# A second MLP on one core: another order of transfers, and the remainder's units at two fixed places

## Chip, core and metric

The kernel runs on one core of a Trainium2 chip. The metric is the device time of one execution in microseconds (us). Three runs of the kernel before gave 961.51 us (median), 959.44 and 965.2 us.

## What is computed

Windowed attention with 32 global tokens in each of 4 batches and 8 heads gives 2176 token rows of 512 features. A gated MLP (RMS norm, 512 to 1536 to 512) and a second MLP follow:

```python
h = x @ w_in                     # 512 -> 2048
g = np.maximum(0.01 * h, h)
return (g @ w_out).astype(np.float32)   # 2048 -> 512
```

All of it is float32. To keep that accuracy each operand of a large product is split into a rounded high half (ScalarE cast) and a residual (VectorE subtract), and a product is three matmuls: high by high, low by high, high by low (`mm3`).

## The kernel before, in words

The change lies in the second MLP, the last 360 us or so. Its 2176 columns are 128 left over ("the rest") and two halves `s` of 1024. A half takes 8 up steps `up`, `j` = 0 to 7, one for each pair of hidden chunks, and then 8 down steps `dn`; 32 steps `g` in all.

An up step makes four blocks of hidden values by seven products of six matmuls each instead of eight (Strassen's scheme in Winograd's form). They run in the order 1, 6, 7, 5, 2, 4, 3. TensorE writes them to PSUM tiles `px`, `pw`, `py`, `pz`; VectorE adds them up (`u`, `v`, `h`), ScalarE copies `x` and applies the leaky ReLU (once on `h[:, 0]` behind product 2, once on the other three blocks behind product 3). Between the products the same engines prepare the next step's weights (`make_w`, places 0 to 2). In half 0 these are 128x768 and 128x1024 splits of `q`, which VectorE first extends by four sums; the finished operands `wr` (1792 KB) are also stored to DRAM (`keep_parts`), and half 1 loads them back (`fetch_w`). In a down step `make_w` splits the raw output weights, and `dop_of` splits the hidden values that are the stationary operands `d`. A `dop` ring of six buffers serves `d` and the rest's weights `rw`.

The rest is worked on in 32 units beside the up steps: unit `u` loads 256 KB (`rest_load`, two `raw` buffers), splits them into `rw` (`rest_split`), and multiplies with three matmuls into `pr` or `po` (`rest_step`). Units 0 to 15 are its first layer, with a turn of four transposes behind every fourth; units 16 to 31 its second, for which every fourth unit also needs a split of the rest's hidden values, `hr`.

The order on TensorE, VectorE, ScalarE and the SP queue is that of the code in this part (a manual schedule). Before it a scheduler places instructions. All transfers go out from SP in program order. An SP transfer whose source or buffer isn't ready holds up those behind it.

Before, `BESIDE` says how many units run in an up step (none in the first, three in the next two, then two), part of them behind product 7 and part behind product 4. A unit ends with the split of the unit two later and the load of the one four later. Behind product 4 SP gets the store of the next operands and then the load of a later `q`. In half 0 the columns for half 1 are loaded (`columns_in`) at the end of a down step and split (`columns_made`) at the end of the next.

Of the kernel before, what the change touches and what calls it, by code (L numbers as in the profile page):

```python
# [24 lines left out]
def tile_window_global_attention_two_mlps(  # L25
# [595 lines left out]


    PAIRS = NF2 // 2
    pre2, rings, ys2, w_in, w_out = [], [], {}, {}, {}

    def rows(c0, n):

# [55 lines left out]
    def keep_parts(j):  # L683
        nc.sync.dma_start(out=w2_dram[j], in_=w_in[0, j].bitcast(F32).rearrange("p y s c -> p y (s c)"))

    def quarter():
        return pre2[0].tile([P, 8, HK], F32, tag="q", name="q")

    def weight_pair(j):

        raws = []

        def make():
            q = quarter()
            for s, f, r in zip((0, 2), (j + PAIRS, j), raws):
                v = q[:, s:s + 2].rearrange("p s c -> p (s c)")
                narrow(mp, v, r, f"b0_{f}")
                nc.sync.dma_start(out=w2_f32[f][0], in_=v)
            weight_sums(q)
            for hi, lo, r in weight_parts(j):  # L700
                split(hi, lo, q[:, r])
            keep_parts(j)
        return [lambda: raws.extend(raw2(f, 0) for f in (j + PAIRS, j)), make]
# [23 lines left out]
    def ahead():  # L727

        ph_at.close()
        pre2.append(ctx.enter_context(tc.tile_pool(name="pre2", bufs=1, side="right", reuse_waits="tile")))  # L730

        jobs = one_ahead([narrowed(f, 0) for j in range(1, PAIRS - 4) for f in (j, j + PAIRS)] + [weight_pair(0)])
        for x, (k, d) in enumerate((k, d) for k in range(KC // 2) for d in range(0, HALF, HK)):
            jobs.insert(2 + 2 * x, lambda k=k, d=d: columns_made(0, k, d, columns_in(0, k, d)))
        return jobs

    def columns_in(s, k, d):

# [153 lines left out]
    rings.extend((pre2[0], wp2))  # L892
    ND = 6
    NU = 2 * NS * PAIRS
    wq, wfs, dops, hid = {}, {}, {}, {}

    def lone(name):

# [6 lines left out]
    def kind(g):  # L905
        s, r = divmod(g, 2 * PAIRS)
        return (s, *divmod(r, PAIRS))

    def load_q(j):

        if j < PAIRS:
            q = wq[j] = quarter() if j % 2 else wp2.tile([P, 8, HK], F32, tag=f"h{PAIRS - 1}", name=f"q{j}")
            for s, f in ((0, j + PAIRS), (2, j)):
                nc.sync.dma_start(out=q[:, s:s + 2].rearrange("p s c -> p (s c)"), in_=w2_f32[f][0])

    def fetch_w(g):

# [13 lines left out]
    def make_w(g, place):  # L931

        if g >= NU:
            return
        s, layer, j = kind(g)
        if layer:
            if place == 0:
                high(w_out[g][:, 0], wfs[g])
            elif place == 1:
                low(w_out[g][:, 1], wfs[g], w_out[g][:, 0])  # L940
        elif s == 0:
            q = wq[j]
            if place == 0:
                wq["parts"] = weight_parts(j)
                high(wq["parts"][0][0], q[:, wq["parts"][0][2]])
                weight_sums(q)
            elif place == 1:
                low(wq["parts"][0][1], q[:, wq["parts"][0][2]], wq["parts"][0][0])
                high(wq["parts"][1][0], q[:, wq["parts"][1][2]])
            else:  # L950
                low(wq["parts"][1][1], q[:, wq["parts"][1][2]], wq["parts"][1][0])
                keep_parts(j)
                load_q(j + 2)


# [23 lines left out]

    def rest_load(u):  # L980

        if u >= NRU + NF2:
            return
        raw = rest["raw", u] = wp2.tile([P, HALF], F32, tag="raw", bufs=2, name=f"raw{u}")
        if u < NRU:
            fq, kc = divmod(u, KC)
            nc.sync.dma_start(out=raw.rearrange("p (f c) -> p f c", c=P), in_=w2_fours[fq][:, :, kc * P:(kc + 1) * P])
        else:
            nc.sync.dma_start(out=raw, in_=w2_f32[u - NRU][1])

    def rest_split(u):

        if u < NRU + NF2:
            t = rest["w", u] = halves_tile(f"rw{u}")
            split(t[:, 0], t[:, 1], rest.pop(("raw", u)))
            rest_load(u + 2)

    def rest_cols(u):

        if NRU <= u < NRU + NF2 and u % 4 == 0:  # L1000
            t = rest["h"] = wp2.tile([P, 2, 4, P], F32R, tag="yr", name=f"hr{u}")
            split(t[:, 0], t[:, 1], rest["hid"][:, u - NRU:u - NRU + 4])

# [4 lines left out]
    def rest_second():  # L1008
        rest["y"] = wp2.tile([P, 2, KC, P], F32R, tag="yr", name="yr")
        split(*(rest["y"][:, h].rearrange("p k c -> p (k c)") for h in range(2)), rest["y32"])  # L1010
        rest["hid"] = wp2.tile([P, NF2, P], F32, tag="hid", name="hid")
        rest_split(0)
        rest_split(1)

    def rest_third():
        rest_cols(NRU)
        rest_split(NRU)
        rest_split(NRU + 1)

    def rest_turn(fq, hn):  # L1020
        pt = lone(f"pt{fq}")
# [4 lines left out]
    def rest_step(u):  # L1026
        w = rest.pop(("w", u))
        turn = rest.pop("turn", None)
        if u < NRU:
            fq, kc = divmod(u, KC)  # L1030
            if kc == 0:
                rest["p"] = lone(f"pr{fq}")
            mm3(rest["p"], [rest["y"][:, h, kc] for h in range(2)], [w[:, h] for h in range(2)], kc == 0, kc == KC - 1)
            if kc == KC - 1:
                hn = wp2.tile([P, HALF], F32, tag="hn", name=f"hn{fq}")
                leaky(hn, rest["p"])
                rest["turn"] = (fq, hn)
        else:
            f = u - NRU
            if f == 0:  # L1040
                rest["p"] = lone("po")
            mm3(rest["p"], [rest["h"][:, h, f % 4] for h in range(2)], [w[:, h] for h in range(2)], f == 0, f == NF2 - 1)
            if f == NF2 - 1:
                ob = wp2.tile([P, DM], F32, tag="hn", name="obr")
                nc.scalar.copy(ob, rest["p"])
                store_rows(0, ob)
        if turn:
            rest_turn(*turn)
        if u < NRU - 2 or u >= NRU:
            rest_cols(u + 1)  # L1050
            rest_split(u + 2)

    units = [lambda u=u: rest_step(u) for u in range(NRU + NF2)]


    BESIDE = {0: (0, 3, 3, 2, 2, 2, 2, 2), 1: (2,) * 8}

    def rest_run(s, j, place):

        n = BESIDE[s][j]  # L1060
        for _ in range(n // 2 if place else n - n // 2):
            units.pop(0)()


    SLOTS = ((0, 0), (0, 1), (1, 0), (1, 1))

# [7 lines left out]

    def up(g):
        s, _, j = kind(g)
        fetch_w(g + 1)
        h = hid[s, j] = wp2.tile([P, 4, HALF], F32, tag=f"h{j}", name=f"h{s}_{j}")
        x1, u2, v = [wp2.tile([P, HALF], F32, tag=x, name=f"{x}{s}_{j}") for x in ("x1", "u2", "v")]
        bx, bw, by = [bank(f"p{c}{s}_{j}") for c in "xwy"]  # L1080
# [4 lines left out]
        product(s, j, 7, by)  # L1085
        plus(v, u2, by)
        make_w(g + 1, 0)
        rest_run(s, j, 0)
        bz = bank(f"pz{s}_{j}")
        product(s, j, 5, bz)  # L1090
        plus(h[:, 3], v, bz)
        make_w(g + 1, 1)
        product(s, j, 2, bx, False)
        leaky(h[:, 0], bx)
        if j == PAIRS - 1:
            dop_of(s, 0)
            dop_of(s, 1)
        product(s, j, 4, by, False)
        plus(h[:, 1], u2, by)
        make_w(g + 1, 2)  # L1100
        if (s, j) == (0, 0):
            rest_second()
        rest_run(s, j, 1)
        product(s, j, 3, bz, False)
        plus(h[:, 2], u2, bz)
        leaky(h[:, 1:4], h[:, 1:4])

    def out_tile(s, t, last):
        ob = wp2.tile([P, DM], F32, tag=("x1", "u2", "v")[t % 3], name=f"ob{s}_{t}")
# [6 lines left out]
    def dn(g):  # L1116
# [6 lines left out]
        def unit(t, x):  # L1123
# [2 lines left out]
            mm3(dn.op[t], [d[:, h, t % 4 * P:(t % 4 + 1) * P] for h in range(2)], [w_out[g][:, h, f] for h in range(2)],  # L1126
                (j, f) == (0, 0), (j, f) == (PAIRS - 1, 1))

        if j < PAIRS - 1:
            for x, (f, n) in enumerate(SLOTS):  # L1130
                dop_of(s, 4 * j + x + 2)
                if x == 2:
                    make_w(g + 1, 0)
                for t in range(4 * n, 4 * n + 4):
                    unit(t, x)
                if x == 2:
                    make_w(g + 1, 1)
        else:
            for x in (2, 3):
                dop_of(s, 4 * j + x)  # L1140
            if s == 0:
                rest_third()
            make_w(g + 1, 0)
            for n, t in enumerate(range(NT2 - 1, -1, -1) if s else range(NT2)):
                for x in range(4):
                    if SLOTS[x][1] == t // 4:
                        unit(t, x)
                out_tile(s, t, n)
        if s + 1 < NS and 1 <= j < 6:
            if j > 1:  # L1150
                columns_made(*dn.columns)
            if j < 5:
                k, d = divmod(j - 1, 2)
                dn.columns = (s + 1, k, d * HK, columns_in(s + 1, k, d * HK))

    with tc.manual_schedule(engines={mybir.EngineType.PE, mybir.EngineType.DVE, mybir.EngineType.Activation,
                                     mybir.EngineType.SP}):
        load_q(1)
        load_q(2)
        rest_first()  # L1160
        rest_load(0)
        rest_load(1)
        for g in range(NU):
            (dn if kind(g)[1] else up)(g)

# [58 lines left out]
```

## Time and profile before

| | us |
|---|---|
| median of three runs | 961.51 |
| profiled execution | 963.23 |
| its span, first to last instruction | 961.5 |
| TensorE busy | 925.0 (96%) |
| VectorE busy | 585.5 (61%) |
| ScalarE busy | 461.0 (48%) |

The profile lists instructions by engine (PE is TensorE, DVE VectorE, ACT ScalarE, SP SyncE with the queue) with start and duration, and for idle time what ended it. TensorE's weight loads have a line of their own (PEld). A matmul's end is modelled; the step from one matmul's start to the next shows the pace.

### The profile page before, as it was taken

The page shows a single profiled execution, that of the slowest core. Times are in us where ns is not written, and L with a number is a line of the kernel's source. Part 1 is how long each engine was busy: PE and PEld are TensorE (multiplying, and loading weights), DVE is VectorE, ACT ScalarE, POOL GpSimd, SP SyncE. Part 2 cuts the span into 40 slices and gives each one's busy share as a digit, 9 for nine tenths or more (in the row PEclk, how much of TensorE's full clock was granted, in tenths as well). Part 3 has the DMA queues.
Part 4 walks back from the last instruction along what each step waited for, and adds up shares of the span by engine and source line. Part 5 has one row for each costly group of instructions (what it writes and reads, how often), then busy time and mean ns, then how long its engine had stood idle before and what let it go on. Part 6 is the DMA issues. An engine that isn't in the chain of part 4 may idle for free.

```text
span 961.5 us, 14038 instructions
## 1 busy us (share of the span) xinstructions
PE 925.0 (96%) x5056; PEld 755.1 (79%) x5056; DVE 585.5 (61%) x1216; ACT 461.0 (48%) x958; POOL 4.5 (0%) x26
## 2 busy tenths in 40 slices
PE   6799999999999999999999999899999999999998
PEld 4557777777777777777999999778788788888886
DVE  5689985596666887443577833666545634445332
ACT  5886774664554655333454422455433523434222
POOL 1000000000000000000000000000000000000000
PEclk9899999999999999999999999999999999999999
DMA  9587994876769999744789992678422275641113
GB/s 306 174 283 262 312 365 149 276 271 228 254 220 379 349 355 339 277 135 146 281 265 329 316 348 74 223 252 278 164 66 88 66 264 214 229 168 55 44 49 106
DMA packets 87174, 215.37 MB, mean 224 GB/s; under 512 B 11456, under 2 KB 25280, under 8 KB 85056
## 3 DMA queue, kind: packets, MB, share of 16 engines
q1 hardware_dynamic: 87104, 214.47, 64.6%
q8 instruction: 40, 0.66, 0.3%
q14 instruction: 30, 0.25, 0.1%
HBM read 154.14 MB, written 60.29 MB: 223 GB/s over the span
## 4 chain that ended last, share of the span: by engine, by line
PE 71%; DMA 10%; DVE 4%; ACT 3%; issue 1%; SPq 1%; DVEq 0%; ACTq 0%
PE o L78 15%; PE pg L78 12%; PE yp L78 11%; PE pv L78 11%; PE px L78 3%; PE pz L78 3%; PE py L78 3%; PE po L146 2%; PE sc L146 2%; DMA raw<-w_fours 2%; PE pw L78 2%; DMA y_dram<-ys 2%; PE pp L255 2%; DMA q<-y_dram 2%; DMA wr<-w_f 2%
## 5 line engine op out<-in xcount | busy, mean ns | idle before, releaser
L78 PE MATMUL o<-wr,d 128*128 128x512 f32 x768 | 175.6, 390 | 2.8 <-ACT d L82 1.5
L78 PEld LDWEIGHTS o<-wr,d 128*128 128x128 f32 x768 | 143.8, 188 | 34.4 <-ACT d L82 1.9
L78 PE MATMUL pg<-xh,w 128*128 128x512 f32 (+1 forms) x464 | 132.6, 367 | 1.8 <-DMA w<-w_dram 1.4
L78 PE MATMUL pv<-xh,w 128*128 128x512 f32 (+1 forms) x464 | 129.6, 361 | 0.0
L78 PE MATMUL yp<-hsh,w 128*128 128x512 f32 (+1 forms) x480 | 124.0, 365 | 2.0 <-ACT hsh L82 1.4
L78 PEld LDWEIGHTS yp<-hsh,w 128*128 128x128 f32 x480 | 83.6, 188 | 16.0 <-ACT hsh L82 2.7
L78 PEld LDWEIGHTS pg<-xh,w 128*128 128x128 f32 x464 | 80.8, 188 | 19.3 <-issue 5.6
L78 PEld LDWEIGHTS pv<-xh,w 128*128 128x128 f32 x464 | 82.2, 188 | 11.5 <-issue 1.3
L78 PE MATMUL pg<-xl,w 128*128 128x512 f32 (+1 forms) x232 | 83.2, 359 | 0.0
L78 PE MATMUL pv<-xl,w 128*128 128x512 f32 (+1 forms) x232 | 83.0, 358 | 0.0
L82 ACT CAST w<-wf 128x512 fp32r<-128x512 f32 x92 | 56.6, 616 | 43.2 <-PE yp L78 22.6
L235 ACT ACTIVATE s_ring<-s_ring,mx 128x224 f32<-128x224 f32 x128 | 60.3, 472 | 30.4 <-DVE mx L232 30.1
L78 PE MATMUL yp<-hsl,w 128*128 128x512 f32 (+1 forms) x240 | 74.8, 361 | 0.0
L85 DVE TENSOR_TENSOR w<-wf,w 128x512 fp32r<-128x512 f32 x92 | 62.9, 685 | 16.2 <-ACT w L82 16.1
L85 DVE TENSOR_TENSOR wr<-wr 128x1024 fp32r<-128x1024 f32 x16 | 19.6, 1225 | 67.2 <-ACT wr L82 67.0
L82 ACT CAST hsh<-th 128x512 fp32r<-128x512 f32 (+1 forms) x60 | 33.3, 556 | 48.8 <-DVE th L829 48.1
L829 DVE SCALAR_TENSOR_TENSOR th<-th,pv 128x512 f32<-128x512 f32 (+1 forms) x60 | 36.2, 603 | 30.4 <-PE pv L78 29.8
L78 PE MATMUL pz<-ysb,wr 128*128 128x512 f32 x192 | 49.4, 393 | 2.2 <-DVE h L967 2.2
L82 ACT CAST wr<-wr 128x1024 fp32r<-128x1024 f32 x16 | 16.8, 1051 | 68.8 <-DMA wr<-w_f 56.1
L85 DVE TENSOR_TENSOR d<-h,d 128x512 fp32r<-128x512 f32 x64 | 41.1, 685 | 13.9 <-ACT d L82 13.7
L78 PEld LDWEIGHTS pg<-xl,w 128*128 128x128 f32 x232 | 43.5, 188 | 6.6 <-DVE xn L497 0.3
L78 PEld LDWEIGHTS yp<-hsl,w 128*128 128x128 f32 x240 | 43.7, 188 | 6.1 <-DVE nr L108 0.3
(160 smaller groups left out, 1468.9 us busy)
## 6 DMA issues: line engine op xcount, KB each, us to landing
w<-w_dram SPq DMA_DIRECT2D x84, 512.0 KB, 6.1
w<-w SPq DMA_DIRECT2D x36, 512.0 KB, 5.7
w_dram<-w SPq DMA_DIRECT2D x36, 512.0 KB, 4.1
w64b<-w SPq DMA_DIRECT2D x32, 512.0 KB, 6.4
wf<-w_f SPq DMA_DIRECT2D x60, 256.0 KB, 4.4
w_dram<-wr SPq DMA_DIRECT2D x8, 1792.0 KB, 6.7
wr<-w_dram SPq DMA_DIRECT2D x8, 1792.0 KB, 7.4
kq<-kqv SPq DMA_DIRECT2D x32, 352.0 KB, 5.5
```

What stands on the lines that cost most here:

```text
L78: nc.tensor.matmul(dst, lhs[a], rhs[b], start=first and i == 0, stop=last and i == 2, skip_group_check=onto)
L82: nc.scalar.copy(hi, src)
L85: nc.vector.tensor_tensor(out=lo, in0=src, in1=hi.bitcast(F32), op=ALU.subtract)
L146: x = nc.tensor.matmul(dst, lhs, rhs, start=start, stop=stop)
L235: x = nc.scalar.activation(out=sp, in_=sp, func=AF.Exp, bias=mx[:, c:c + 1], scale=-1.0, accum_out=sm[:, c:c + 1])
L255: nc.tensor.transpose(pp[:, n * P:(n + 1) * P], s[:, c0:c0 + P], ident)
L829: nc.vector.scalar_tensor_tensor(out=t, in0=t, scalar=0.5, in1=pp[1][:, 0:n], op0=ALU.mult, op1=ALU.mult)
```

## The change

Loads of a step go first in the SP queue and the store of its operands last: `up` begins with the two `raw` loads of its own two units, then `fetch_w`, then the store, which moves from the step before. The two units run behind product 4 and behind product 3 of every up step, the first step included. Their splits stand in the same step: the first behind product 2, the second behind product 4. The split of `hr` follows that of its unit. At the end of the last up step of a half three `d` splits are made (before: two, behind product 2), and in down steps `d` is split three ahead instead of two. The columns for half 1 are now loaded at the start of a down step and split in the same step. One load of `q` moves into the jobs of the first MLP, whose scheduler then places a few instructions differently.

```diff
-        return jobs
+        return jobs + [lambda: load_q(1)]
...
                 low(wq["parts"][1][1], q[:, wq["parts"][1][2]], wq["parts"][1][0])
-                keep_parts(j)
                 load_q(j + 2)
...
     def rest_split(u):
-        if u < NRU + NF2:
-            t = rest["w", u] = halves_tile(f"rw{u}")
-            split(t[:, 0], t[:, 1], rest.pop(("raw", u)))
-            rest_load(u + 2)
-
-    def rest_cols(u):
-
-        if NRU <= u < NRU + NF2 and u % 4 == 0:
+        t = rest["w", u] = halves_tile(f"rw{u}")
+        split(t[:, 0], t[:, 1], rest.pop(("raw", u)))
+        if u >= NRU and u % 4 == 0:
             t = rest["h"] = wp2.tile([P, 2, 4, P], F32R, tag="yr", name=f"hr{u}")
             split(t[:, 0], t[:, 1], rest["hid"][:, u - NRU:u - NRU + 4])
...
-        if u < NRU - 2 or u >= NRU:
-            rest_cols(u + 1)
-            rest_split(u + 2)
...
-    BESIDE = {0: (0, 3, 3, 2, 2, 2, 2, 2), 1: (2,) * 8}
...
     def up(g):
         s, _, j = kind(g)
+        u = 2 * (s * PAIRS + j)
+        if (s, j) == (0, 0):
+            rest_first()
+        for x in range(2):
+            rest_load(u + x)
+        if g == 0:
+            load_q(2)
         fetch_w(g + 1)
+        if s == 0 and j:
+            keep_parts(j)
...
         make_w(g + 1, 0)
-        rest_run(s, j, 0)
...
         leaky(h[:, 0], bx)
-        if j == PAIRS - 1:
-            dop_of(s, 0)
-            dop_of(s, 1)
+        if (s, j) == (0, 0):
+            rest_second()
+        rest_split(u)
         product(s, j, 4, by, False)
         plus(h[:, 1], u2, by)
         make_w(g + 1, 2)
-        if (s, j) == (0, 0):
-            rest_second()
-        rest_run(s, j, 1)
+        rest_split(u + 1)
+        rest_step(u)
         product(s, j, 3, bz, False)
         plus(h[:, 2], u2, bz)
+        if j == PAIRS - 1:
+            for x in range(3):
+                dop_of(s, x)
         leaky(h[:, 1:4], h[:, 1:4])
+        rest_step(u + 1)
...
+        own = s + 1 < NS and 1 <= j < 5
+        if own:
+            k, d = divmod(j - 1, 2)
+            q = columns_in(s + 1, k, d * HK)
...
-                dop_of(s, 4 * j + x + 2)
+                dop_of(s, 4 * j + x + 3)
                 if x == 2:
                     make_w(g + 1, 0)
+                elif x == 3 and own:
+                    columns_made(s + 1, k, d * HK, q)
```

The steady up step of half 0, here j = 3. TensorE before (`pr<-rw` is a unit, numbers tell the tiles apart):

```order
L78 MATMUL px_3_6704<-ysa_5373,wr_6624 128x512 x6
L78 MATMUL pw_3_6705<-ysa_5373,wr_6624 128x512 x6
L78 MATMUL py_3_6706<-ysa_5373,wr_6624 128x512 x6
L78 MATMUL pr_6640<-rw_6650,yr 128x512 x3
L78 MATMUL pz_3_6742<-ysb_5376,wr_6624 128x512 x6
L78 MATMUL px_3_6704<-ysb_5376,wr_6624 128x512 x6
L78 MATMUL py_3_6706<-ysb_5376,wr_6624 128x512 x6
L78 MATMUL pr_6640<-rw_6687,yr 128x512 x3
L78 MATMUL pz_3_6742<-ysb_5376,wr_6624 128x512 x6
```

TensorE now, at the same step:

```order
L78 MATMUL px_3_6694<-ysa_5365,wr_6624 128x512 x6
L78 MATMUL pw_3_6695<-ysa_5365,wr_6624 128x512 x6
L78 MATMUL py_3_6696<-ysa_5365,wr_6624 128x512 x6
L78 MATMUL pz_3_6724<-ysb_5368,wr_6624 128x512 x6
L78 MATMUL px_3_6694<-ysb_5368,wr_6624 128x512 x6
L78 MATMUL py_3_6696<-ysb_5368,wr_6624 128x512 x6
L78 MATMUL pr_6664<-rw_6741,yr 128x512 x3
L78 MATMUL pz_3_6724<-ysb_5368,wr_6624 128x512 x6
L78 MATMUL pr_6664<-rw_6755,yr 128x512 x3
```

The unit that stood behind product 7 (the first `py`) now stands behind product 4 (the second `py`), the other behind product 3. VectorE at that step, before (`wr<-q` and `rw<-raw` are residuals):

```order
L967 TENSOR_TENSOR v_3_6703<-u_3_6702,py_3_6706 128x512
L672 TENSOR_TENSOR q_6577<-q_6577 128x256 x4
L85 TENSOR_TENSOR rw_6737<-raw_6653,rw_6737 128x512
L967 TENSOR_TENSOR h_3_6700<-v_3_6703,pz_3_6742 128x512
L85 TENSOR_TENSOR wr_6728<-q_6577,wr_6728 128x768
L967 TENSOR_TENSOR h_3_6700<-u_3_6702,py_3_6706 128x512
L85 TENSOR_TENSOR wr_6728<-q_6577,wr_6728 128x1024
L85 TENSOR_TENSOR rw_6776<-raw_6690,rw_6776 128x512
L967 TENSOR_TENSOR h_3_6700<-u_3_6702,pz_3_6742 128x512
```

VectorE now:

```order
L966 TENSOR_TENSOR v_3_6693<-u_3_6692,py_3_6696 128x512
L672 TENSOR_TENSOR q_6569<-q_6569 128x256 x4
L966 TENSOR_TENSOR h_3_6690<-v_3_6693,pz_3_6724 128x512
L85 TENSOR_TENSOR wr_6718<-q_6569,wr_6718 128x768
L85 TENSOR_TENSOR rw_6741<-raw_6685,rw_6741 128x512
L966 TENSOR_TENSOR h_3_6690<-u_3_6692,py_3_6696 128x512
L85 TENSOR_TENSOR wr_6718<-q_6569,wr_6718 128x1024
L85 TENSOR_TENSOR rw_6755<-raw_6687,rw_6755 128x512
L966 TENSOR_TENSOR h_3_6690<-u_3_6692,pz_3_6724 128x512
```

Before, the residuals made in this step (6737, 6776) are read two units later; now they (6741, 6755) are read by the units of this very step. ScalarE in half 1 at j = 2, a step with an `hr` split, now (before, `hr` and its unit were cast in the step ahead of it):

```order
L1061 COPY x_2_7899<-px_2_7902 128x512
L969 ACTIVATE h_2_7898<-px_2_7902 128x512
L82 CAST rw_7941<-raw_7892 128x512
L82 CAST hr_7944<-hid 128x512
L82 CAST rw_7954<-raw_7894 128x512
L969 ACTIVATE h_2_7898<-h_2_7898 128x1536
```

The casts of the step's units stand behind the leaky ReLU on product 2 (`h<-px`), so they begin when that product is done. The SP queue at steps 3 and 4 of half 0, before (`w_dram<-wr` is the store):

```order
L684 DMA w_dram_123<-wr_6624 128x3584
L914 DMA q<-w_fours_103 128x512
L914 DMA q<-w_fours_101 128x512
L987 DMA raw_6690<-w_fours_102 128x4x128
L987 DMA raw_6740<-w_fours_102 128x4x128
L684 DMA w_dram_124<-wr_6728 128x3584
L914 DMA q_6768<-w_fours_103 128x512
```

The SP queue now:

```order
L694 DMA q<-w_fours_103 128x512
L694 DMA q<-w_fours_101 128x512
L984 DMA raw_6685<-w_fours_101 128x4x128
L984 DMA raw_6687<-w_fours_101 128x4x128
L684 DMA w_dram_123<-wr_6624 128x3584
L694 DMA q_6752<-w_fours_103 128x512
L694 DMA q_6752<-w_fours_101 128x512
```

The store no longer stands ahead of the `q` and `raw` loads of its turn but behind them.

## Rows read from the trace of the kernel before

**Rows 1.** The page's busy times: TensorE, its weight loads, other engines.

```profile
PE 925.0 (96%) x5056; PEld 755.1 (79%) x5056; DVE 585.5 (61%) x1216; ACT 461.0 (48%) x958; POOL 4.5 (0%) x26
```

**Rows 2.** Stretches: from:to, length, busy by engine, granted clock, DMA share, GB/s.

```profile
597.20:691.10 93.90, 90.02 (x398) 72.78 (x396) 60.25 (x99) 44.73 (x62) 0.00 (x0) 1.00 0.72 237
...
782.20:870.30 88.10, 87.99 (x389) 72.31 (x388) 41.26 (x62) 32.50 (x47) 0.00 (x0) 1.00 0.55 203
...
612.00:623.00 11.00, 8.41 (x35) 6.15 (x34) 7.43 (x13) 3.87 (x6) 0.00 (x0) 1.00 0.58 164
```

**Rows 3.** TensorE's timeline: start, length, tiles, count, idle before and releaser.

```profile
563.68 0.56 PE L78 MATMUL pg<-xh,w 128*128 128x320 f32 x2 [1.41 <-DMA w<-w_dram]
...
618.13 1.23 PE L78 MATMUL pr<-rw,yr 128*128 128x512 f32 x3 [1.68 <-ACT rw L82]
620.27 1.63 PE L78 MATMUL pz<-ysb,wr 128*128 128x512 f32 x6 [0.91 <-DVE h L967]
...
634.09 1.66 PE L78 MATMUL pz<-ysb,wr 128*128 128x512 f32 x6 [1.28 <-DVE h L967]
...
692.58 0.50 PE L78 MATMUL o<-wr,d 128*128 128x512 f32 x1 [1.46 <-ACT d L82]
693.44 65.39 PE L78 MATMUL o<-wr,d 128*128 128x512 f32 x287 [0.36 <-DVE d L85]
759.30 0.73 PE L78 MATMUL o<-wr,d 128*128 128x512 f32 x2 [0.47 <-ACT wr L82]
760.55 21.80 PE L78 MATMUL o<-wr,d 128*128 128x512 f32 x94 [0.52 <-DVE wr L85]
```

**Rows 4.** The chain that ended last, its transfers: start, length to landing, which.

```profile
610.66 7.58 DMA raw<-w_fours
...
681.12 7.00 DMA wr<-w_f
...
786.86 7.14 DMA wr<-w_dram
```

**Rows 5.** TensorE's timeline inside up steps of half 0 and half 1.

```profile
661.91 0.84 PE L78 MATMUL pr<-rw,yr 128*128 128x512 f32 x3
...
663.96 1.52 PE L78 MATMUL px<-ysb,wr 128*128 128x512 f32 x6
665.32 1.52 PE L78 MATMUL py<-ysb,wr 128*128 128x512 f32 x6
...
811.17 1.52 PE L78 MATMUL px<-ysb,wr 128*128 128x512 f32 x6
```

**Rows 6.** ScalarE's timeline in two up steps of half 0.

```profile
632.62 1.04 ACT L82 CAST wr<-q 128x1024 fp32r<-128x1024 f32 x1
633.57 0.59 ACT L970 ACTIVATE h<-px 128x512 f32<-128x512 f32 x1
...
664.30 1.06 ACT L82 CAST wr<-q 128x1024 fp32r<-128x1024 f32 x1 [2.04 <-DVE q L672]
```

**Rows 7.** VectorE's timeline at the end of an up step of half 0.

```profile
678.85 1.22 DVE L85 TENSOR_TENSOR wr<-q,wr 128x1024 fp32r<-128x1024 f32 x1
679.99 0.68 DVE L85 TENSOR_TENSOR rw<-raw,rw 128x512 fp32r<-128x512 f32 x1
680.59 0.68 DVE L967 TENSOR_TENSOR h<-u,pz 128x512 f32<-128x512 f32 x1
```

**Rows 8.** ScalarE's timeline in two up steps of half 1.

```profile
812.73 0.60 ACT L970 ACTIVATE h<-px 128x512 f32<-128x512 f32 x1 [3.78 <-PE px L78]
813.22 0.61 ACT L82 CAST rw<-raw 128x512 fp32r<-128x512 f32 x1
...
825.65 0.62 ACT L82 CAST hr<-hid 128x512 fp32r<-128x512 f32 x1 [1.44 <-PE po L78]
```

**Rows 9.** First up step: TensorE's product 4, then ScalarE's row beside it.

```profile
604.05 1.52 PE L78 MATMUL py<-ysb,wr 128*128 128x512 f32 x6
...
604.67 0.59 ACT L970 ACTIVATE h<-px 128x512 f32<-128x512 f32 x1
```

More of the change, by code (lines that the diff above doesn't have):

```diff
@@ L623, in tile_window_global_attention_two_mlps @@
     PAIRS = NF2 // 2
-    pre2, rings, ys2, w_in, w_out = [], [], {}, {}, {}
+    pre2, rings, ys2, w_in, w_out, wq = [], [], {}, {}, {}, {}
     def rows(c0, n):
@@ L687, in quarter, with load_q @@
         return pre2[0].tile([P, 8, HK], F32, tag="q", name="q")
+    def load_q(j):
+        if j < PAIRS:
+            q = wq[j] = quarter() if j % 2 else rings[1].tile([P, 8, HK], F32, tag=f"h{PAIRS - 1}", name=f"q{j}")
+            for s, f in ((0, j + PAIRS), (2, j)):
+                nc.sync.dma_start(out=q[:, s:s + 2].rearrange("p s c -> p (s c)"), in_=w2_f32[f][0])
     def weight_pair(j):
@@ L894, in tile_window_global_attention_two_mlps @@
     NU = 2 * NS * PAIRS
-    wq, wfs, dops, hid = {}, {}, {}, {}
+    wfs, dops, hid = {}, {}, {}
     def lone(name):
@@ L907, in kind @@
         return (s, *divmod(r, PAIRS))
[L909 to L914, printed above, removed]
     def fetch_w(g):
@@ L980, in rest_load @@
     def rest_load(u):
-        if u >= NRU + NF2:
-            return
         raw = rest["raw", u] = wp2.tile([P, HALF], F32, tag="raw", bufs=2, name=f"raw{u}")
@@ L1011, in rest_second @@
         rest["hid"] = wp2.tile([P, NF2, P], F32, tag="hid", name="hid")
[L1012 to L1018, printed above, removed]
     def rest_turn(fq, hn):
@@ L1048, in rest_step @@
             rest_turn(*turn)
-        if u < NRU - 2 or u >= NRU:
-            rest_cols(u + 1)
-            rest_split(u + 2)
-    units = [lambda u=u: rest_step(u) for u in range(NRU + NF2)]
-    BESIDE = {0: (0, 3, 3, 2, 2, 2, 2, 2), 1: (2,) * 8}
[L1058 to L1062, printed above, removed]
     SLOTS = ((0, 0), (0, 1), (1, 0), (1, 1))
@@ L1138, in dn @@
         else:
[L1139 to L1143, printed above, removed]
+            dop_of(s, 4 * j + 3)
             for n, t in enumerate(range(NT2 - 1, -1, -1) if s else range(NT2)):
@@ L1148, in dn @@
                 out_tile(s, t, n)
[L1149 to L1154, printed above, removed]
     with tc.manual_schedule(engines={mybir.EngineType.PE, mybir.EngineType.DVE, mybir.EngineType.Activation,
                                      mybir.EngineType.SP}):
[L1158 to L1162, printed above, removed]
         for g in range(NU):
```

## Prediction, written before the changed kernel ran

> **What bounds the kernel now.** I read the busy times first: TensorE works 925.0 of 961.5 us, every other engine far less [rows 1]. Only its idle time and its work can move the end, and the change takes no matmul away. Next, the stretches. The up steps of half 0 leave TensorE idle 3.9 of 93.9 us, those of half 1 only 0.1 of 88.1 [rows 2]. Then TensorE's timeline, to see who ended each idle time of the second MLP [rows 3]. Seven waits of any size stand there: 1.68, 0.91 and 1.28 around units of the rest in early up steps, 1.46 and 0.36 where the down steps of half 0 begin, 0.47 and 0.52 at a later down step. They add up to 6.68 us; everything else runs without a gap. Last the chain that ended last names the transfers behind such waits: a `raw` load took 7.58 us to land, the first output weights 7.00 [rows 4]. The order rows show the `raw` loads behind a store of 1792 KB, and by the code the store of the last operands goes out ahead of the output weights too. So the second MLP has at most some 7 us to give, and the question is what the new places of the splits cost.
>
> **What the change takes away.** With the loads ahead of the store the `raw` of a step is on its way before the store is, and the first output weights as well; the columns' load, which by the code stood at the end of a down step behind a split and ahead of the next `fetch_w`, now follows `fetch_w` at the step's start. I take all seven waits as gone: -6.7 us [rows 3]. Some may survive, at least the wait of a queue that stays busy, so from -5 to -6.7. What is late next is worked out now.
>
> **What the splits cost.** No instruction is added: the same 32 units with the same splits run. But a unit's split now stands in its own step. In-order engines make a chain: product 2 ends, ScalarE runs the leaky ReLU, then casts `rw`; VectorE takes the residual; only then can the unit's third matmul (high by low) start. TensorE has one product to do meanwhile. Let E be the end of product 2. A product takes 1.36 us, so a matmul 0.227 [rows 5], and the unit's third matmul is due at E + 1.36 + 0.45 = E + 1.81. Before, the split was two units ahead and this chain covered.
>
> *Half 1, steps without `hr` (four).* ScalarE starts 0.20 after the product (811.17 + 1.36 to 812.73) and the next instruction 0.49 later, a cast lasting 0.61 [rows 5, 8]. The cast ends at E + 1.30, the residual runs 0.68 [rows 7] to E + 2.01, the matmul starts at about E + 2.05. Wait 0.25 each, 1.0 in all.
>
> *Half 1, steps with `hr` (four).* ScalarE casts `hr` (0.62) behind `rw`, to E + 1.80 [rows 8]. VectorE makes the residual of `rw` first, from E + 1.33, and that of `hr` from E + 1.93 (one follows another after 0.60 [rows 7]) to E + 2.61. The unit's second matmul wants it: due at E + 1.59, started at E + 2.66. Wait 1.07 each, 4.3 in all.
>
> *Half 0, steps 1 to 6.* ScalarE comes later still. The cast of the 1024-column weights waits for VectorE's sums and began 2.39 after product 7 (661.91 to 664.30), and the next instruction comes 0.95 behind such a cast [rows 5, 6]. Before, a unit stood between products 7 and 5; now E is only two products, 2.73, behind product 7. So the leaky ReLU starts at E + 0.61 instead of E + 0.20, the cast of `rw` at E + 1.10, its residual at E + 1.74, and the third matmul at E + 2.47: wait 0.65. VectorE then has `h`, the 1024-column residual (1.14 until the next, [rows 7]) and the second unit's residual, which ends at E + 4.76. Product 3 ends at E + 4.06, that unit's third matmul is due at E + 4.51 and starts at E + 4.81: wait 0.30. In steps 2, 4 and 6 four transposes push product 3 back (an estimate from their columns: 4 x 0.227 / 4 = 0.23) and cover this. Three steps at 0.95, three at 0.65: 4.8. Step 7 has no sums; it costs 0.25 like the quiet steps of half 1.
>
> *The first step.* Before it had no unit. ScalarE's leaky ReLU begins at 604.67 [rows 9]; then come the casts of `yr` (605.16) and `rw` (605.65 to 606.26), the residual of `yr` from 605.8, that of `rw` from 606.4 to 607.08. The third matmul is due at 604.05 + 1.36 + 0.45 = 605.86 and starts at 607.13: 1.27. The second unit adds 0.30 as above. 1.6 in all. The loads are not what is late: they go out before the `q` load that stood ahead of them.
>
> *The two ends of the up steps.* The first `d` residual now stands behind the last `h` addition, which waits for product 3. That addition starts 0.2 after the product, the residual 0.60 later, done at 1.48. TensorE has one unit (0.68) and one matmul (0.23) until then, and wants it at 0.91: wait 0.62, twice, 1.2. Down steps otherwise gain slack, since `d` is split three ahead.
>
> Sum: 1.0 + 4.3 + 4.8 + 0.25 + 1.6 + 1.2 = 13.2 us of new waits. From below: if ScalarE were not held by the weights' cast (half 0: 2.65 instead of 5.05), an `hr` step waited only for its cast (0.45 each), and the first step and the ends cost half, 13.2 falls to about 7. From above: a `raw` load that lands as late as the 7.58 of [rows 4], counted from half a us into the step, comes at 8.1, while the cast in half 0 is due at 5 x 1.36 + 1.10 = 7.9; with the queue still busy some 0.6 per step over seven steps, 4.2 more. I take 13.2, since its durations are those of the same instructions.
>
> *Other parts.* Half 1's second step needs operands whose load took 7.14 us and arrived just in time [rows 4]. Two `raw` loads now stand ahead of it, but no longer ahead of the output stores, and the unit before it waits 1.07 longer anyway; I cost it at nothing, and at 1 us if the stores aren't sooner. In the first MLP the scheduler moved a 512 KB weight load behind the first store; there a wait of 1.41 already stands at 563.68 [rows 3]. I take +0.5, from -1.4 (it goes) to +2 (it doubles and a little more).
>
> Net: 13.2 - 6.7 + 0.5 = +7.0 us. On the profiled execution's 963.23 this is 970.2, and on the median of the three runs, 1.72 lower, 968.5.
>
> *A rule against the change, weighed.* In the stretch 612 to 623, where TensorE was busy for 8.41 of 11 us, the granted clock stayed 1.00, the level of 2.4 GHz [rows 2]; the new waits are shorter and leave each step fuller than that. If the clock fell to 1.2 GHz over one up step, its 48 matmuls would take 48 x 0.227 = 10.9 us more. The Trainium skill, page "TensorE: Matmul & The Clock Gate", section "A second HAM failure mode: psum-queue depth-cycling", says that frequent micro-idles between groups of matmuls can make the clock swing between its two levels. By that rule, one step in four falling would give some 44 us more; by the row, nothing.
>
> **Rivals.**
> - *Faster.* The late loads were the only thing that counted, and the splits hide: VectorE delivers each residual by E + 1.81. For it: VectorE is idle a third to a half of these stretches, ScalarE more [rows 2]. Against: their order, since the cast stands behind the leaky ReLU on product 2. It would take a cast that starts at E + 0.4 at the latest. Then -6.7 + 0.5, so 955.3.
> - *Gains and costs nearly cancel.* The lower bound above: 7 to 8 of new waits, net +1 to +2, 963. For it: VectorE's sums may run earlier, since a unit's residual no longer stands beside them. Against: they follow `v`, which waits for product 7.
> - *The loads become late.* The `raw` loads go out only at the step's start, behind a 512 KB `q` load, where before they went out a step ahead. If they land at 8.1 or later, 4.2 us more than my sum: 972.7. Against: in the new order the store ahead of them has had most of a step to finish.
> - *The clock falls* in some up steps: 979 for a single one.
> That the change does not do what it says is excluded by the order rows.
>
> **How the numbers follow.** Forecast 0.59 (own range 965 to 972); cancelling 0.22; late loads 0.12; faster 0.05; clock 0.02. Differences under 0.5% (4.8 us) can't be told from no change. Slower by more: most of the forecast (0.50), late loads and clock (0.14), a little of the cancelling case (0.02), together 0.66. Within: 0.09 + 0.20 = 0.29. Faster: 0.05. The range, 962.5 to 974, takes in the cancelling case and the late loads and leaves out the faster one and the clock.
>
> **What would show it.** Right: TensorE's row for the third matmul of a unit (`pr<-rw`, `po<-rw`) shows idle time ended by VectorE's `rw` or ScalarE's, in nearly every up step, about 1 us with `hr` and 0.25 without in half 1, 0.65 to 0.95 in half 0; the first `o` matmul waits about 0.6 for VectorE's `d`; the waits at 618, 634, 692 and 759 are gone. Half 1's up steps together grow from 88.1 to about 93 us. Wrong: no idle time before those matmuls, or waits released by the `raw` load rather than by the cast.

## The result and the profile after

The changed kernel took 969.19 us (median of 19 runs), the kernel before 962.16 beside it (19 runs): a ratio of 1.0069, 95% interval 1.0052 to 1.0086. The difference of the medians is +7.0 us, what was forecast; the interval lies above 1.005, so the change is slower. The profiled execution took 967.52, its span 965.7.

The busy times answer [rows 1]:

```profile
PE 931.8 (96%) x5056; PEld 753.4 (78%) x5056; DVE 587.0 (61%) x1216; ACT 461.5 (48%) x958; POOL 4.5 (0%) x26
```

TensorE runs the same 5056 matmuls and is "busy" 6.8 us longer. So part of the new waiting stands inside busy rows, which matters below.

The stretches answer [rows 2]; first half 0's up steps, then half 1's, then the eleven us whose clock was read before:

```profile
594.40:690.80 96.40, 94.04 (x398) 71.83 (x397) 62.54 (x102) 46.09 (x66) 0.00 (x0) 1.00 0.65 225
778.60:873.80 95.20, 92.19 (x389) 71.29 (x389) 41.87 (x63) 33.67 (x50) 0.00 (x0) 1.00 0.56 199
612.00:623.00 11.00, 10.75 (x45) 7.94 (x45) 7.23 (x13) 5.76 (x8) 0.00 (x0) 1.00 0.66 223
```

Half 1's up steps grew from 88.1 to 95.2, half 0's from about 95.4 to 96.4. The granted clock stayed at 1.00.

TensorE's timeline, where [rows 3] had the seven waits (start, length, what, idle time before it):

```profile
603.50 1.31 PE L78 MATMUL pr<-rw,yr 128*128 128x512 f32 x3 [0.77 <-ACT rw L82]
...
651.81 1.22 PE L78 MATMUL pr<-rw,yr 128*128 128x512 f32 x3 [0.25 <-ACT rw L82]
...
690.81 0.39 PE L78 MATMUL o<-wr,d 128*128 128x512 f32 x1
691.68 87.13 PE L78 MATMUL o<-wr,d 128*128 128x512 f32 x383 [0.48 <-DVE d L85]
...
792.10 1.67 PE L78 MATMUL px<-ysa,wr 128*128 128x512 f32 x6 [0.66 <-DMA wr<-w_dram]
...
812.28 0.50 PE L78 MATMUL po<-rw,hr 128*128 128x512 f32 x1 [0.35 <-ACT hr L82]
813.09 0.73 PE L78 MATMUL po<-rw,hr 128*128 128x512 f32 x2 [0.31 <-DVE hr L85]
```

The waits at 618, 634, 692 and 759 are gone; the down steps of half 0 run 383 matmuls without a gap. In their place stand waits for the casts `rw` and `hr` and for residuals: printed in steps 0 to 6 of half 0 and in the `hr` steps of half 1, while step 7 of half 0 and the steps of half 1 without `hr` print none.

One step of half 1 without `hr`, on all engines, answers [rows 5, 7, 8]; product 2 is the first row:

```profile
797.72 1.52 PE L78 MATMUL px<-ysb,wr 128*128 128x512 f32 x6
799.08 1.52 PE L78 MATMUL py<-ysb,wr 128*128 128x512 f32 x6
799.28 0.60 ACT L969 ACTIVATE h<-px 128x512 f32<-128x512 f32 x1 [4.82 <-PE px L78]
799.77 1.13 ACT L82 CAST rw<-raw 128x512 fp32r<-128x512 f32 x2
800.42 0.69 DVE L85 TENSOR_TENSOR rw<-raw,rw 128x512 fp32r<-128x512 f32 x1 [1.81 <-ACT rw L82]
800.44 1.23 PE L78 MATMUL po<-rw,hr 128*128 128x512 f32 x3
801.16 0.19 PEld L78 LDWEIGHTS po<-rw,hr 128*128 128x128 f32 x1 [0.43 <-DVE rw L85]
801.50 1.56 PE L78 MATMUL pz<-ysb,wr 128*128 128x512 f32 x6
```

With E = 799.08 the leaky ReLU starts at E + 0.20, the cast at E + 0.69, the residual at E + 1.34 and ends at E + 2.03: within 0.02 of the forecast chain. What follows was not in it: the residual is waited for by a weight load (E + 2.08, on PEld), and the matmul comes behind that. The unit's three matmuls stretch to 1.06 (800.44 to 801.50) where three take 0.68, and no idle time is printed. That is where the busy time grew.

In half 0 ScalarE is held by the weights' cast, as in [rows 6], here with E = 650.04. The first step is alike (leaky ReLU at 601.84 with E = 601.21), except that the cast of `yr` (602.33) stands ahead of that of `rw` (602.83), as [rows 9] led to expect:

```profile
649.71 1.05 ACT L82 CAST wr<-q 128x1024 fp32r<-128x1024 f32 x1 [3.11 <-DVE q L672]
650.66 0.59 ACT L969 ACTIVATE h<-px 128x512 f32<-128x512 f32 x1
651.15 1.13 ACT L82 CAST rw<-raw 128x512 fp32r<-128x512 f32 x2
```

The leaky ReLU comes at E + 0.62, the cast at E + 1.11 (forecast 0.61 and 1.10), without a gap and without a wait for `raw`. The chain that ended last has these transfers among others, against [rows 4]:

```profile
619.64 4.29 DMA raw<-w_fours
...
783.45 8.61 DMA wr<-w_dram
```

A `raw` load that took 7.58 takes 4.29, but 7.58 was one of the slow ones: by the medians from 600 to 680 us (below) it is the `q` loads that gain most. The operands of half 1's second step, 7.14 before, now take 8.61 and are waited for.

**By pace.** Where rows hide waits, the starts of product 1 (`px` from `ysa`) tell a step's whole length:

```profile
594.39 1.55 PE L78 MATMUL px<-ysa,wr 128*128 128x512 f32 x6
606.99 1.56 PE L78 MATMUL px<-ysa,wr 128*128 128x512 f32 x6
619.02 1.55 PE L78 MATMUL px<-ysa,wr 128*128 128x512 f32 x6
631.20 1.52 PE L78 MATMUL px<-ysa,wr 128*128 128x512 f32 x6
...
803.60 1.53 PE L78 MATMUL px<-ysa,wr 128*128 128x512 f32 x6
815.72 1.52 PE L78 MATMUL px<-ysa,wr 128*128 128x512 f32 x6
827.00 1.52 PE L78 MATMUL px<-ysa,wr 128*128 128x512 f32 x6
```

A step with two units and no wait takes 7 x 1.36 + 2 x 0.68 = 10.88, and 11.37 with four transposes; before has many at just these lengths. Down steps without a wait take 87.04 in half 0 (they do in two kernels below). Above that:

| stage | before: length, lost | after: length, lost |
|---|---|---|
| half 0, up | 95.36, 6.8 | 96.42, 7.9 |
| half 0, down | 89.62, 2.6 | 87.83, 0.8 |
| half 1, up | 88.13, 0.6 | 95.16, 7.6 |
| half 1, first `o` matmul to the end | 91.2, 0 | 91.9, 0.8 |
| second MLP, first product to the end | 364.3, 10.0 | 371.3, 17.1 |

So the change took 10.0 us of waits away and made 17.1. The rest of the program can't be read from one pair of traces: the second MLP starts at 597.22 before and 594.39 after, but see the first MLP below.

### The profile page after: what moved, and what is told of

Its sections match the earlier page's. It is cut to its first block, busy times and chain, and to the rows that moved or that the text cites. A ratio compares the mean times of both kernels' runs of the same rounds, so it can differ in the third digit from the quotient of the medians.

```text
span 965.7 us, 14059 instructions
## 1 busy us (share of the span) xinstructions
PE 931.8 (96%) x5056; PEld 753.4 (78%) x5056; DVE 587.0 (61%) x1216; ACT 461.5 (48%) x958; POOL 4.5 (0%) x26
## 4 chain that ended last, share of the span: by engine, by line
PE 73%; DMA 7%; DVE 5%; ACT 4%; issue 2%; SPq 1%; DVEq 0%; ACTq 0%
PE o L78 17%; PE yp L78 12%; PE pg L78 12%; PE pv L78 11%; PE px L78 3%; PE pz L78 3%; PE po L146 2%; PE py L78 2%; PE sc L146 2%; DMA y_dram<-ys 2%; PE pw L78 2%; PE pp L255 2%; DMA q<-y_dram 1%; DMA raw<-w_fours 1%; PE po L78 1%
## 5 line engine op out<-in xcount | busy, mean ns | idle before, releaser
L82 ACT CAST d<-h 128x512 fp32r<-128x512 f32 x64 | 38.4, 620 | 39.9 <-PE o L78 39.9
L832 DVE SCALAR_TENSOR_TENSOR th<-th,pg 128x512 f32<-128x512 f32 (+1 forms) x58 | 34.7, 599 | 21.5 <-ACT th L831 21.1
```

Of the source, the lines that this page charges most:

```text
L82: nc.scalar.copy(hi, src)
L832: x = nc.vector.scalar_tensor_tensor(out=t, in0=t, scalar=1.0, in1=gate, op0=ALU.add, op1=ALU.mult)
```

## Experiments

Theory: the transfer order gains, and the splits in their units' own step, behind product 2's leaky ReLU, cost more. Rivals: the loads are what is late; single units at two places cost by themselves; the first MLP matters. "Second MLP" in what follows is the span less the start of the first product 1. Each ratio is to the kernel before, run beside it.

| kernel | second MLP | median us | ratio, 95% interval |
|---|---|---|---|
| before / after | 364.3 / 371.3 | 962.16 / 969.19 | 1.0069, 1.0052 to 1.0086 |
| store_back | 382.1 | 980.31 | 1.0184, 1.0155 to 1.0214 |
| before_store_last | 356.7 | 952.95 | 0.9901, 0.9874 to 0.9927 |
| cast_early | 360.6 | 957.90 | 0.9965, 0.9940 to 0.9991 |
| hr_ends | 368.0 | 964.93 | 1.0036, 1.0016 to 1.0055 |
| ahead | 363.8 | 960.97 | 0.9990, 0.9962 to 1.0018 |
| ahead2 | 360.8 | 957.03 | 0.9947, 0.9927 to 0.9967 |
| early_all | 358.1 | 954.41 | 0.9924, 0.9894 to 0.9954 |
| best | 354.8 | 951.71 | 0.9901, 0.9874 to 0.9927 |
| before_q1 | 363.8 | 963.20 | 1.0011, 0.9991 to 1.0030 |
| before_again | 363.5 | 959.57 (one run) | none |

**The transfer order by itself: before_store_last and store_back.** In the kernel before, the store alone moves:

```
# make_w, place 2
-                keep_parts(j)
                 load_q(j + 2)
# up, behind fetch_w(g + 1)
+        if s == 0 and j:
+            keep_parts(j)
```

> The kernel before with one edit: the store of the operands goes out at the start of the next step, behind the loads; splits and units stay where they were. Theory (the change's transfer order is good and its split places are bad): the waits of 1.68, 0.91, 1.28, 1.46 and 0.36 at 618 to 692 shrink or go, by the steps' lengths 4 to 7 us less than the kernel before, 955 to 958. Rival (the waits are those of three units in one step, whatever the store does): 961 to 962.

It gained 7.6 us in the second MLP, a little above the expected 4 to 7, and is 0.99 of before. None of the waits of 618 to 692 is left; only 0.52 and 0.53 at 748, where the columns are split. The same edit backwards in the changed kernel is store_back.

> The changed kernel with the store of the operands back at the end of the step, ahead of the q load, so ahead of the next step's raw loads: the transfer order alone undone. Theory: raw loads land 6 to 8.5 us into a step of half 0 where the cast is due at 7.9, and the first output weights come late again: 1 to 4 us more than the changed kernel, 970 to 973, with waits ended by loads of raw or w. Rival (order of transfers doesn't matter once splits are late): 969 with no such waits.

It lost 10.8 in the second MLP, far above the 1 to 4. Its transfers from 600 to 680 us (KB each, median us to landing), then the same of after and of before:

```profile
w_dram<-wr SPq DMA_DIRECT2D x6, 1792.0 KB, 6.9
raw<-w_fours SPq DMA_DIRECT2D x12, 256.0 KB, 7.9
q<-w_fours SPq DMA_DIRECT2D x10, 256.0 KB, 8.0
```

```profile
w_dram<-wr SPq DMA_DIRECT2D x6, 1792.0 KB, 8.8
raw<-w_fours SPq DMA_DIRECT2D x14, 256.0 KB, 4.5
q<-w_fours SPq DMA_DIRECT2D x10, 256.0 KB, 3.8
```

```profile
w_dram<-wr SPq DMA_DIRECT2D x6, 1792.0 KB, 6.7
raw<-w_fours SPq DMA_DIRECT2D x16, 256.0 KB, 5.0
q<-w_fours SPq DMA_DIRECT2D x11, 256.0 KB, 7.8
```

In store_back the loads land as late as was thought. In after the store takes longer instead, and nothing in these steps waits for it. The size was missed in step 7, 17.72 us long where after has 11.28; the 4.4 that are left are just above the expected range. ScalarE and TensorE there, in store_back:

```profile
694.95 1.04 ACT L82 CAST wr<-wr 128x1024 fp32r<-128x1024 f32 x1 [8.13 <-DMA wr<-w_f]
695.90 0.59 ACT L970 ACTIVATE h<-px 128x512 f32<-128x512 f32 x1
696.38 1.13 ACT L82 CAST rw<-raw 128x512 fp32r<-128x512 f32 x2
697.05 1.65 PE L78 MATMUL pr<-rw,yr 128*128 128x512 f32 x3 [4.12 <-ACT rw L82]
```

The cast of the first output weights stands ahead of the units' casts in ScalarE's order and waited 8.13 for its load. The wait hit a unit that has nothing to do with those weights, and behind it the granted clock was lower too (last section).

**The place of the splits: cast_early.** Loads, store and unit places of the changed kernel stay; only this moves:

```
         plus(h[:, 3], v, bz)
+        rest_split(u)
         make_w(g + 1, 1)
         ...
         leaky(h[:, 0], bx)
-        rest_split(u)
```

> The changed kernel with the split of a step's first unit (and hr) put behind product 5's addition, ahead of product 2's leaky ReLU, in the same step; loads where they are. Theory: the waits of 0.4 (half 1) and 1.24 (with hr) go, those of half 0 shrink to the second unit's 0.3 in three steps, the first step keeps about 1 us for yr: 9 to 11 us less than the changed kernel, 958 to 960. Rival 1 (raw loads land late): the cast is due 2.4 us sooner in the step, so it meets the load: no gain or a loss, 969 or more, with waits that a load ends. Rival 2 (unit places): 969.

10.7 us came back. The steps of half 1 from the second on are 11.02 and then 10.88, steps 1 to 6 of half 0 11.23 to 11.41: 0.35 is left in the three steps for the second unit, as forecast. The earlier cast does meet the `raw` load: in six of half 0's eight steps ScalarE waits 0.91 to 2.67 for it. The longest of these waits, and TensorE's product 1 of its step and of the next:

```profile
658.65 0.62 ACT L82 CAST rw<-raw 128x512 fp32r<-128x512 f32 x1 [2.67 <-DMA raw<-w_fours]
```

```profile
653.05 1.53 PE L78 MATMUL px<-ysa,wr 128*128 128x512 f32 x6
...
664.28 1.55 PE L78 MATMUL px<-ysa,wr 128*128 128x512 f32 x6
```

This step takes 11.23, and so does the one whose wait is 1.67; TensorE prints no wait in steps 1 to 7. So the load was there 5.6 us into the step, where the changed kernel's cast comes at 7.9. This refutes late `raw` loads as the cause of the waits in these steps, and most of the unit places. Half 1's first step is the exception: it stayed at 13.64 (13.46 in after). There the cast waits 1.33 for its load, and TensorE 0.24 for the `x` copy and 0.88 for the `w` load.

**Two terms alone: hr_ends.**

```
# the hr split: out of rest_split, behind the last unit of the step before
         rest_step(u + 1)
+        rest_cols(u + 2)
# the first d split of a half
         rest_split(u)
+        if j == PAIRS - 1:
+            dop_of(s, 0)
```

> The changed kernel with two edits that the trace tells apart: each hr split goes behind the last unit of the step before (that of unit 16 into the last down step of half 0), and the first d split of a half goes ahead of product 4's addition in the last up step. Theory (in-order ScalarE and VectorE: what stands ahead of a split sets the wait): the half 1 steps with hr come from 12.12 to the 11.28 of the others, 0.84 each in four steps, so 3.4; the wait of 0.48 ahead of the first o matmul goes, by the steps' lengths 0.64 each, 1.3: 4.7 in all, about 964.5. Rival (the residual of rw, not hr, sets the wait in those steps): steps stay at 12.12, 968.

The steps with `hr` went from 12.12 to 11.28 to 11.31, the 0.84 that was expected. Half 0's down steps went from 87.83 to 87.04, so an end cost 0.79. In all 3.3 instead of 4.7, since half 1's first step became 0.67 longer: its `x` copy waited for output stores (TensorE lost 0.60 there), and its `w` load landed later against the work (1.32 instead of 0.66).

**Splits a whole step ahead: ahead and ahead2.** Loads and splits for units u + 2 and u + 3 in the step that runs u and u + 1:

```
+            rest_load(u + 2)
+            rest_load(u + 3)
         ...
-        rest_split(u)
+            rest_split(u + 2)
         ...
-        rest_split(u + 1)
+            rest_split(u + 3)
```

> The changed kernel with the splits one step ahead of their units (units 2 to 15 and 18 to 31) and each hr split one step ahead; loads, store, unit places and the first step's two units stay. Theory (a split in its unit's own step, behind product 2's leaky ReLU, is what costs): of the 17.4 us by which the changed kernel's up steps and their ends are longer than their matmuls, the first step's 1.7, the two ends' 1.3 and the 0.8 for a weight load in half 1 stay, and some 13.5 go, so about 955.5 us, below the kernel before as well. Rival 1 (the transfer order or late raw loads make the waits): loads go out a step ahead as well, so it too forecasts a gain here, but at the price of no other waits; it is told apart by cast_early, where the loads stay. Rival 2 (the places of the units between products 4 and 3 and behind 3 cost by themselves): still about 969.

It missed by 5.5 us. The quiet steps are at 10.88, but three places lost: 1.0 in step 2, where step 1 had four splits to do, and 5.1 in half 1's first two steps. TensorE's timeline, then two stretches of it:

```profile
621.68 1.42 PE L78 MATMUL pw<-ysa,wr 128*128 128x512 f32 x5 [0.71 <-DVE wr L85]
...
789.64 2.15 PE L78 MATMUL px<-ysa,wr 128*128 128x512 f32 x6 [2.51 <-DMA wr<-w_dram]
```

```profile
789.60:791.60 2.00, 1.96 (x7) 1.54 (x8) 0.00 (x0) 0.00 (x0) 0.00 (x0) 0.75 0.93 377
791.60:794.10 2.50, 2.50 (x8) 1.99 (x7) 0.00 (x0) 0.59 (x1) 0.00 (x0) 0.52 0.89 378
```

The `w` load was queued behind two `raw` loads. After the wait of 2.51 the granted clock was 0.75 and 0.52, and the step was 12.61 long, 1.73 above 10.88. In ahead2 these two loads go out in the last down step of half 0:

```
             for x in range(2):
                 rest_split(NRU + x)
+                rest_load(NRU + x + 2)
```

> ahead with one edit: the raw loads of units 18 and 19 go out in the last down step of half 0, right behind the splits of units 16 and 17, not at the start of half 1 ahead of the w load. Theory (in ahead a w load that is queued behind two raw loads lands late, TensorE waits 2.51 and then runs nine matmul pairs at a granted clock of 0.5 to 0.75): half 1's first two steps come from 14.79 and 12.61 to some 11.5 and 10.9, 5 us less than ahead, about 956, and the clock stays at 1.00 there. Rival (the w load is late because the output stores hold the queue): the wait stays above 1.5, 960.

The wait for `w` and the slow clock went, but only 3.0 of the 5 came back, since at half 1's first step another wait took the place:

```profile
781.36 0.58 ACT L1068 COPY x<-px 128x512 f32<-128x512 f32 x1 [2.18 <-DMA out<-ob]
782.00 1.67 PE L78 MATMUL px<-ysb,wr 128*128 128x512 f32 x6 [1.44 <-ACT x L1068]
```

The `x` copy writes a buffer that an output tile used, and so waits for its store. So the rival was right in part: at this boundary the output stores count too.

**All waits for splits away, singles kept: early_all.** It is cast_early with the edits of hr_ends (the first `d` split right behind the leaky ReLU), the split of `yr` ahead of product 2, and the `raw` loads of units 16 and 17 in the last down step of half 0.

> cast_early with what the traces say is left of the waits taken away: hr split a step ahead, the first d split behind product 2's leaky ReLU, the split of yr ahead of product 2 as well, the raw loads of units 16 and 17 in the last down step of half 0. Units, store and loads else as in the changed kernel. Theory (only the place of the splits costs): from the second MLP's 360.6 in cast_early the ends give 1.6, half 1's first step some 2, the first step 0.5 to 1, to 356, that is 953, as good as the best of the other order; three steps of half 0 keep 0.35 for their second unit. Rival (two single units per step cost something by themselves): 957 or more.

954.41, and the second MLP 358.1, 2.1 above the expected 356 (half 1's first step kept 1.4 us, 0.64 of it again for the `x` copy). The `w` load is no longer waited for. It is the `raw` loads ahead of it that count, as the queue shows in hr_ends and then here. The output stores leave the queue free at nearly the same place, 4.6 and 4.7 us into half 1:

```profile
783.58 0.93 SPq L986 DMA_DIRECT2D raw<-w_f  x2
784.61 0.38 SPq L929 DMA_DIRECT2D wr<-w_dram  x1
```

```profile
783.57 0.41 SPq L929 DMA_DIRECT2D wr<-w_dram  x1
```

The `w` load goes out 4.7 us into the half instead of 5.6, TensorE wants it at about the same place (12.7 and 12.8), and the wait for it, 1.32 in hr_ends, is gone.

The rival's 957 or more is refuted: single units at fixed places cost little once their operands are split early.

**The two good parts together: best.** before_store_last with the changed kernel's columns (loaded at the start of their down step, split ahead of its last group):

```
+        own = s + 1 < NS and 1 <= j < 5
+        if own:
+            q = columns_in(s + 1, k, d * HK)
         ...
+                elif x == 3 and own:
+                    columns_made(s + 1, k, d * HK, q)
```

> before_store_last and the changed kernel's place for the columns (loaded at the start of their down step and split in it): the order of transfers without the late splits. Theory: the waits of 0.52 and 0.53 at 748 go, and the down steps of half 0 come from 89.1 to 87.8: 1.3 us less than before_store_last's 953, about 951.7. Rival (the columns' load at the step's start delays the next output weights, as it goes out behind them only by the queue): 953 or more, with a wait for w.

The down steps of half 0 are at 87.04, the second MLP at 354.8. The median is 1.2 below before_store_last's; the two intervals are the same, so only the traces tell these two apart. It beats both kernels: 0.9901 of before.

**The first MLP: before_q1 and before_again.**

```
# first MLP's job list
+        return jobs + [lambda: load_q(1)]
# ahead of the second MLP
-        load_q(1)
```

> The kernel before with the first q load issued among the first MLP's jobs, as in the changed kernel; the second MLP is as before. Theory 1 (this takes the wait of 1.41 for a w load in the first MLP, which the changed kernel's trace lacks): 1 to 2 us less, 959 to 960. Theory 2 (the first MLP differs from one execution to another; before_store_last lacks that wait too, with the same order there): no difference, 961 to 962.

> The kernel before once more, unchanged, for a second trace. If the waits of the first MLP belong to the program, the 1.41 for a w load stands again and the second MLP starts at 597.2; if they belong to the execution, it starts up to 4 us sooner, as in the trace of before_store_last. The second MLP takes 364.2 from its first product to the end in either case.

before_q1's ratio holds 1 within its interval: no gain or loss of its own that can be told. before_again is the same program as before, and its trace has the wait at 0.36 instead of 1.41, and the start at 594.30 instead of 597.22:

```profile
560.76 0.57 PE L78 MATMUL pg<-xh,w 128*128 128x320 f32 x2 [0.36 <-DMA w<-w_dram]
...
594.30 1.55 PE L78 MATMUL px<-ysa,wr 128*128 128x512 f32 x6
```

So the part ahead of the second MLP differs by 3 us from one execution to another (over all twelve traces the start lies between 592.77 and 600.85, the last in early_all, whose profiled execution took 960.7 against its median of 954.41), and no reading of it from one trace stands. The second MLP differed by 0.8 (363.5 to 364.3).

## Why the prediction was right, and where its sizes were off

The result and the mechanism came as forecast: the gain of the transfers is real, and the new chains (product 2, leaky ReLU, cast, residual, third matmul) cost more than it. That the sum came out within 1 us (969.19, forecast 968.5) was luck: two errors cancelled, new waits 3.9 too small and removed waits 3.3 too small.

| term | forecast | by pace |
|---|---|---|
| half 1, steps without `hr`, each | 0.25 | 0.40 |
| half 1, steps with `hr`, each | 1.07 | 1.24 |
| half 0, odd steps, each | 0.95 | 1.09 to 1.15 |
| half 0, even steps, each | 0.65 | 0.81 to 0.83 |
| half 0, step 7 | 0.25 | 0.40 |
| first step | 1.6 | 1.72 |
| each end of the up steps | 0.62 | 0.79 |
| `w` load of half 1's second step | 0 | 0.7 to 0.8 |
| new waits, sum | 13.2 | 17.1 |
| waits removed | 6.7 | 10.0 |
| first MLP | +0.5 | not resolved |

- **New waits: each step about 0.15 too small.** Chains were right to 0.02 in the two steps shown; the weight load that stands between the residual and its matmul was left out (PEld 801.16, waiting for `rw`, in the rows above). The rows point to it as the cause; no run took it away, so its share is not shown. The four transposes take 0.49 by pace, not 0.23; they still cover the second unit, as forecast.
- **The `w` load costed at nothing** waits 0.66, behind two `raw` loads, although its unit waits longer than was forecast. The forecast's alternative of 1 us was the right side: the output stores hold the queue until 782.4, 3.8 us into half 1, and the `raw` loads come between. hr_ends beside early_all shows that without these two loads the wait goes.
- **Removed waits: 10.0, not 6.7.** The idle times of [rows 3] were added up, but a wait also stretches rows that count as busy. The same 5056 matmuls are busy 925.0 before and 922.0 in best, where the second MLP has nearly no wait; these 3.0 fit the missing 3.3, though the rest of the program is in them too, so this is argued and not shown.
- **Loads late?** Not the `raw` loads. But for that `w` load, TensorE's printed waits in the up steps end with a cast or a residual, and the casts follow the leaky ReLU without a gap. `raw` landed in 4.5. What a late load would do is store_back.
- **The sign of being wrong, "no idle time before those matmuls", misleads.** The steps of half 1 without `hr` print none, and those of half 0 print 0.25 where 0.65 to 0.95 were forecast; by pace all of them wait, and longer than forecast. Half 1's up steps grew to 95.2, not to about 93.
- **Faster (955.3).** It wanted the cast at E + 0.4; it starts at E + 0.69 and E + 1.11. cast_early, which puts it ahead of E (at E - 1.20 in the step shown), does go below before.
- **Clock.** It stayed at 1.00 (2.4 GHz) in the up steps, with a wait or two in each: the fall that was weighed against the change did not come. Only longer waits, in ahead and store_back, were followed by a lower one.
- **First MLP.** The forecast +0.5 rested on a wait of 1.41 seen once. It isn't the program's: 0.36 in a second execution.

## What to carry to other kernels

When work is moved to "just before it is needed", count the in-order chain ahead of it on every engine it passes, and let the chain go through the weight load to the matmul. Order a queue by who waits: transfers with a consumer first, stores that nobody waits for last; that alone was worth 1% here, and the schedule change that came with it spent more than that. Compare stages by the starts of a repeated instruction, since idle columns leave out waits inside busy rows.

## What the runs showed that was not expected

- Waits inside busy rows: TensorE's busy time for the same 5056 matmuls was 922.0, 925.0 and 931.8 us in best, before and after.
- The granted clock after a long wait: behind 2.51 us in ahead it was 0.75 and then 0.52 for 4.5 us, together 1.73 us lost; behind 4.12 us in store_back 0.50, the level of 1.2 GHz. In the up steps of after, with waits of 0.25 to 0.77, it was 1.00, and so it was behind single waits of 1.68 in before and 1.86 in store_back. The stretch of store_back behind 4.12:

```profile
697.00:699.00 2.00, 1.95 (x5) 1.41 (x6) 2.00 (x4) 2.00 (x4) 0.00 (x0) 0.50 0.00 0
```

- A store's time to land went with its place in the queue: the same 1792 KB took 6.7 us ahead of the loads (before) and 8.8 behind them (after), and the slower one was the better, as before_store_last (8.3) shows.
